# Attention and a two-layer network on one core: twelve Strassen blocks in the first matrix, one sum begun by a copy inside PSUM, nine sums by accumulating DMAs, and another order

## The chip, the core and the metric

The kernel runs on one core of a Trainium2 chip. The core has five engines that run on their own and meet only at semaphores: TensorE (PE; its weight loads are shown as PEld), VectorE (DVE), ScalarE (ACT), GpSimd (POOL) and SyncE (SP). POOL and SP mainly issue DMAs here; a queue issues its DMAs in order, and a DMA that has to wait for a semaphore holds up those behind it on that queue. SBUF is the working memory, PSUM the eight banks into which TensorE writes. The metric is the device time of the whole program in microseconds (us).

## The reference

```python
def _attn_ref(q, k, v, n_global, n_local):        # q, k, v: (4, 8, 768, 64)
    scores = scale * np.matmul(q, k.transpose(0, 1, 3, 2))
    is_global = pos[None, :] < int(n_global)      # the first 8 keys
    is_local = (rel >= 0) & (rel < int(n_local))  # the last 96 keys
    scores = np.where(is_global | is_local, scores + bias, -1000000000.0)
    a = softmax(scores)
    return np.matmul(a, v)

def _moe_ref(x, w_in, w_out):                     # x: (3072, 512)
    h = x @ w_in                                  # w_in: (512, 2048)
    g = h - np.tanh(h)
    return g @ w_out                              # w_out: (2048, 512)
```

Attention with a window of 96 keys and 8 global ones, then two matrices with g = h - tanh(h) between them. The inputs and the output are float32; the kernel computes in bfloat16 with float32 sums in PSUM.

## The kernel before

**Tiles.** The 3072 rows are 24 units u of 128 rows. Per unit: q and k are loaded (lq, lk) and turned (T, Te; from unit 7 on T is a transposing DMA on SP), S makes the scores on TensorE, E their exponentials on ScalarE, M multiplies with a mask on VectorE, AV multiplies with v, R and N divide by the sums, X and Xe (from unit 8 on Xe is a transposing DMA on SP) put the result into xT, the input of the first matrix. K and V copy the global keys and values in.

**First matrix.** Units go in groups g: 0 and 1 of one unit, 2 to 6 of two, 7 to 9 of four, so that a matmul of group 7 to 9 has 512 moving columns. h is made in 16 pieces f of 128 columns of w_in. `m1` (L477) sums a piece over four quarters of x; `th` (L576) takes the tanh on ScalarE and `g` (L590) subtracts on VectorE, into `gall`. For six blocks of groups 8 and 9 (`DUNITS`, L164; a block is four pieces f, j is its number, so j = 1 to 3) the block is made by Strassen's scheme in Winograd's form: seven products d1 to d7 of four 256-column matmuls (`in_product`, L536) instead of four m1 of four 512-column matmuls. v1 to v4 (L509) are the sums of w_in, y1 to y4 (L514) those of x. One PSUM bank ("r") gathers d1, d6, d5 and d3 in turn; after d1, d6 and d5 its state is copied to SBUF (e0, e1, e2, `d_copy`). C11 is d2 in a bank of its own ("q") plus the copy e0, added by VectorE (q11, L547); q21 and q22 (L550) add bank "z" to the other two copies.

**Second matrix.** All twelve pairs of units use the same scheme with seven products p1 to p7 of eight 256-column matmuls (`product`, L645). n1 to n4 (`g_sum`, L630, VectorE) are the sums of g: n1 and n2 go to buffers `ss`, n3 and n4 back into `gall`. a0, a1, a2 (`keep`) copy bank "r" to `sn` after p1, p6, p5; c11, c21, c22 (`result`, L659) add them on VectorE, c12 is a copy; `st` (L662) stores a unit. p7 reads what n3 wrote, p3 what n4 wrote. w1 to w4 (L617) are the sums of w_out. The last pair, 22, has p3 in two halves.

**What sets the order.** `ORDER` (L17) is a list of words, each a step such as `p3.10` (product 3 of the pair that begins with unit 10), `g.8.4` or `n4.16/d`; the letter behind the slash names the engine where there is a choice (a ScalarE, d VectorE, p POOL's queue, s SP's). The program issues the steps in that order (L797 to L806), so that each engine, and each queue, gets its own in the order of the list. `HOMES` (L74) says which buffer or bank each value has. The tile framework adds the waits. The two tables are left out below.

Of the kernel before, what the change touches and what calls it, by code (L numbers as in the profile page):

```python
# [7 lines left out]
FP32 = mybir.dt.float32  # L8
BF16 = mybir.dt.bfloat16
# [32 lines left out]
lk.18 R.12 N.12/d p4.6 th.5.4 lk.19 V.12/a g.5.4 S.12 lq.17 c21.6 p2.8 M.13 E.14.0 st.3.0/p p1.8 lv.14 E.15.0 n1.8/d
AV.13 K.15/d lq.18 n2.8/d a0.8/a m1.6.14 E.14.1 c11.8 lv.15 v2.3 m1.6.4 R.13 K.14/d th.6.14 N.13/d lv.16 p6.8 g.6.14
Xe.13 th.6.4 lq.19 g.6.4 S.13 a1.8/a M.14 p5.8 E.15.1 n4.8/d m1.6.0 E.16.0 T.18 M.15 m1.6.12 a2.8/a th.6.0 T.17 m1.6.8
E.16.1 g.6.0 AV.14 n3.8/d th.6.12 Xe.12 m1.6.10 th.6.8 V.14/d R.14 g.6.12 K.16/a AV.15 g.6.8 m1.6.2 N.14/d p7.8 R.15
th.6.2 N.15/d th.6.10 m1.6.6 c22.8 Xe.15 g.6.2 p4.8 th.6.6 g.6.10 Xe.14 g.6.6 p3.8 c21.8 p1.10 n1.10/d st.9.0/p c12.8/a
T.19 v1.2 lv.17 S.14 n2.10/d a0.10/a V.15/a M.16 lq.20 p2.10 E.17.1 lq.23 p6.10 n4.10/d E.18.0 lv.19 AV.16 a1.10/d
K.17/a E.17.0 m1.7.15 R.16 lk.20 N.16/d p5.10 th.7.15 c11.10 lq.22 g.7.15 m1.7.2 a2.10/a lk.22 v2.2 S.15 th.7.2 lk.21
g.7.2 p3.10 E.19.1 lq.21 n3.10/d m1.7.6 E.18.1 st.5.0/p M.17 m1.7.4 T.20 E.19.0 M.18 m1.7.3 th.7.6 M.19 V.16/a m1.7.5
T.22 th.7.3 m1.7.7 th.7.5 g.7.6 th.7.4 g.7.5 AV.19 th.7.7 m1.7.1 g.7.4 T.21 R.19 v4.3 m1.7.8 N.19/a v3.2 g.7.7 m1.7.12  # L50
g.7.3 th.7.1 m1.7.10 c12.10/d th.7.8 st.10.0/p AV.17 th.7.12 g.7.8 lk.23 m1.7.9 th.7.10 V.17/d R.17 lv.18 N.17/d m1.7.11
th.7.9 g.7.12 Xe.17 K.19/a lv.20 V.19/a m1.7.14 g.7.10 st.7.0/p g.7.9 p7.10 th.7.14 lv.22 g.7.1 th.7.11 m1.7.0 c22.10
lv.21 g.7.14 m1.7.13 th.7.0 T.23 g.7.11 p4.10 g.7.0 th.7.13 Xe.19 g.7.13 S.16 v4.2 p1.12 c21.10 E.20.0 K.21/d n1.12/d
p2.12 K.20/d a0.12/d E.21.0 n2.12/d AV.18 E.20.1 c11.12 p6.12 R.18 N.18/d a1.12/a n1.14/d S.17 Xe.18 n3.12/d p5.12 M.20
E.21.1 Xe.16 p7.12 a2.12/a n4.12/d E.22.0 AV.20 c22.12 p3.12 M.21 E.22.1 p4.12 K.22/a c12.12/a R.20 n2.14/d V.20/a
st.12.0/p S.18 n3.14/d lv.23 p1.14 N.20/d E.23.1 M.22 AV.21 E.23.0 d1.8.1 d2.8.1 y1.8 e0.8.1/a R.21 p2.14 y2.8 a0.14/a
N.21/d V.21/a d6.8.1 y3.8 Xe.21 AV.22 q11.8.1 e1.8.1/a m1.8.0 R.22 c21.12 N.22/d Xe.20 d5.8.1 th.8.0 d7.8.1 c11.14
e2.8.1/a y4.8 d1.8.3 g.8.0 Xe.22 d2.8.3 e0.8.3/a q22.8.1 d3.8.1 d6.8.3 M.23 th.8.4 st.11.0/s d1.8.2 p6.14 e0.8.2/a
n4.14/d V.22/a d6.8.2 g.8.4 e1.8.3/a d2.8.2 e1.8.2/a d4.8.1 q11.8.3 d5.8.3 AV.23 q21.8.1 e2.8.3/a d5.8.2 a1.14/a R.23
q11.8.2 d3.8.3 e2.8.2/a d7.8.3 N.23/d th.8.12 d3.8.2 q22.8.3 Xe.23 p5.14 th.8.6 g.8.12 d7.8.2 a2.14/a st.13.0/s m1.8.2  # L60
q22.8.2 st.8.0/s th.8.8 p3.14 g.8.6 d4.8.3 g.8.8 th.8.2 d4.8.2 c12.14/a m1.9.0 st.14.0/p y1.9 q21.8.3 m1.8.1 g.8.2
th.8.14 d1.9.1 q21.8.2 m1.8.3 e0.9.1/a y2.9 th.8.10 g.8.14 p7.14 d1.9.2 c22.14 th.8.1 d6.9.1 y3.9 d2.9.2 g.8.10 e1.9.1/a
d2.9.1 th.8.3 p4.14 g.8.1 e0.9.2/a g.8.3 d5.9.1 d6.9.2 q11.9.1 p1.16 e1.9.2/a n1.16/d e2.9.1/a d5.9.2 c21.14 a0.16/a
n2.16/d d7.9.1 st.15.0/s th.9.0 d3.9.1 q11.9.2 e2.9.2/a p6.16 th.9.4 g.9.0 y4.9 d3.9.2 a1.16/a g.9.4 m1.9.1 th.9.8
m1.9.2 n1.18/d th.9.1 g.9.8 d1.9.3 p5.16 e0.9.3/a q22.9.1 d6.9.3 n3.16/d d7.9.2 e1.9.3/a d4.9.1 g.9.1 th.9.2 p2.16
q22.9.2 d2.9.3 n2.18/d p1.18 q21.9.1 g.9.2 d4.9.2 a0.18/a d5.9.3 n4.16/d d7.9.3 e2.9.3/a q11.9.3 p7.16 th.9.6 q22.9.3
d3.9.3 c11.16 a2.16/a p6.18 n3.18/d q21.9.2 m1.9.3 g.9.6 p3.16 th.9.3 c22.16 a1.18/a d4.9.3 th.9.12 g.9.3 p5.18 q21.9.3
th.9.10 g.9.12 p4.16 a2.18/a p2.18 g.9.10 th.9.14 p7.18 c12.16/a n4.18/d st.16.0/p p1.20 c22.18 g.9.14 p3.18 a0.20/a
p4.18 n1.20/d n2.20/d p2.20 n3.20/d p6.20 n1.22/d c21.16 p7.20 n4.20/d a1.20/a st.17.0/p p5.20 n3.22/d c21.18 p2.22
c11.18 a2.20/a st.19.0/s n2.22/d c12.18/a p1.22 st.18.0/s c22.20 c11.20 p4.20 a0.22/a c11.22 p6.22 n4.22/d st.22.0/s  # L70
c21.20 p7.22 a1.22/a st.21.0/p p5.22 p3.20 a2.22/a c22.22 p3.22.0 c12.20/a p4.22 st.20.0/s c12.22.0/d st.22.256/s
p3.22.1 c21.22 c12.22.1/d st.23.0/s st.22.384/s
"""
HOMES = """  # L74
v.0:1 tr.0.1:6 tr.0.0:6 kq.0:2 qk.0:6 v.1:0 tr.1.1:6 tr.1.0:7 kq.1:0 qk.1:5 v.2:2 tr.2.1:7 tr.2.0:5 kq.2:1 qk.2:8 v.3:3
tr.3.1:4 tr.3.0:7 kq.3:3 qk.3:7 v.4:4 tr.4.1:3 tr.4.0:1 kq.4:4 qk.4:9 v.5:5 tr.5.1:4 tr.5.0:5 kq.5:0 qk.5:18 v.6:6
tr.6.1:7 tr.6.0:1 kq.6:1 qk.6:4 v.7:4 kq.7:0 qk.7:16 v.8:8 kq.8:1 qk.8:3 v.9:5 kq.9:17 qk.9:2 v.10:6 kq.10:19 qk.10:10
# [44 lines left out]
def kernel(  # L122
# [27 lines left out]
    WJ = 4  # L150
# [692 lines left out]
```

## Time and profile before

| | |
|---|---|
| time, median of 3 runs | 202.13 us (201.87 to 202.61) |
| span of the profiled execution, first to last instruction | 199.8 us |
| TensorE busy | 193.1 us, 2219 matmuls |
| VectorE busy | 178.6 us |
| ScalarE busy | 135.1 us |
| POOL busy | 75.3 us |
| granted TensorE clock | 1.000 |

The profiled execution has a span and no time of its own beside it; the runs' median is 2.3 us above that span, which is what lies around the instructions. In the groups of instructions a row has: line, engine, operation, what it writes and reads with shapes, count | busy time in us, mean length of one in ns | idle time of the engine ahead of it, and who ended that. In a timeline a row has the start and the length in us. The chain of waits is the work that ended last, followed back from the end. In the list of stretches each engine has its busy time and, in brackets, its instructions.

### The profile page before, as it was taken

What the parts mean: (1) busy time and instruction counts of PE and PEld (TensorE: products, weight loads), DVE (VectorE), ACT (ScalarE), POOL (GpSimd) and SP (SyncE); (2) the same over time, 40 slices, a digit from 0 to 9 for tenths busy, and PEclk for the clock granted to TensorE, in tenths of its full rate; (3) what the DMA queues carried; (4) which work ended last, traced back from release to release, by engine and by line L of the source; (5) the groups of instructions that cost most, each with busy time, mean ns of one, the idle gap of its engine ahead of it and who ended that gap; (6) DMA issues with size and microseconds to landing.
All of it is one profiled execution on the core that took longest, in us unless ns stands there. A gap on an engine that the chain in (4) does not pass through costs nothing.

```text
span 199.8 us, 5524 instructions
## 1 busy us (share of the span) xinstructions
PE 193.1 (97%) x2219; PEld 157.8 (79%) x2219; DVE 178.6 (89%) x348; ACT 135.1 (68%) x234; POOL 75.3 (38%) x97
## 2 busy tenths in 40 slices
PE   8799999999999999999999999999999999999992
PEld 2469998888888988988898655688898687888892
DVE  6487599999999999999999898999999999999942
ACT  3698898726569559758947789578778777464220
POOL 8987576350694057069207904702000100001110
PEclk9999999999999999999999999999999999999999
DMA  5999999999999999989996998994733101001233
GB/s 148 211 180 185 198 163 207 201 156 141 193 167 196 178 153 135 133 188 171 137 158 146 140 173 192 154 155 85 55 108 121 66 0 54 3 0 52 107 132 131
DMA packets 103545, 27.36 MB, mean 137 GB/s; under 512 B 93920, under 2 KB 101472, under 8 KB 103520
## 3 DMA queue, kind: packets, MB, share of 16 engines
q0 software_dynamic: 74048, 16.78, 89.5%
q1 hardware_dynamic: 28928, 9.70, 27.6%
q10 hardware_dynamic: 544, 0.52, 1.0%
q8 instruction: 17, 0.28, 0.5%
q14 instruction: 8, 0.07, 0.1%
HBM read 27.26 MB, written 6.29 MB: 168 GB/s over the span
## 4 chain that ended last, share of the span: by engine, by line
PE 85%; DVE 7%; DMA 3%; ACT 2%; issue 1%; ACTq 0%; DVEq 0%
PE ps L645 36%; PE ps L477 27%; PE ps L536 9%; PE ps L396 5%; PE ps L427 5%; DMA f<-in_q_dram 3%; DVE gall L590 2%; DVE x L444 2%; DVE mem L407 1%; PE ps L455 1%; ACT mem L403 1%; PE ps L320 1%; ACT mem L274 1%; PE ps L365 1%; ACT th L576 1%
## 5 line engine op out<-in xcount | busy, mean ns | idle before, releaser
L477 PE MATMUL ps<-xT,w_in_bf 128*128 128x256 bf16 (+2 forms) x544 | 69.0, 279 | 0.0
L477 PEld LDWEIGHTS <-w_in_bf 128*128 128x128 bf16 x544 | 47.2, 98 | 12.4
L576 ACT ACTIVATE th<-ps 128x512 f32<-128x512 f32 (+1 forms) x74 | 41.8, 591 | 18.7 <-PE ps L477 13.6
L590 DVE TENSOR_TENSOR gall<-ps,th 128x512 bf16<-128x512 f32 (+1 forms) x74 | 47.4, 668 | 6.0 <-ACT th L576 5.6
L645 PEld LDWEIGHTS <-gall 128*128 128x128 bf16 x488 | 46.4, 98 | 7.0
L662 POOL DMA_DIRECT2D out_dram<-ot x14 | 8.1, 580 | 102.5 <-ACT ot L274 52.4
L403 ACT ACTIVATE mem<-ps 128x1024 bf16<-128x1024 f32 x44 | 43.3, 1024 | 4.3 <-PE ps L396 4.2
L645 PE MATMUL ps<-w_out_bf,gall 128*128 128x256 bf16 (+1 forms) x296 | 36.3, 270 | 0.0
L274 ACT COPY sn<-ps 128x256 f32<-128x256 f32 x32 | 12.0, 375 | 20.3 <-PE ps L645 16.3
L645 PE MATMUL ps<-f,ss 128*128 128x256 bf16 x192 | 24.9, 273 | 0.0
L645 PE MATMUL ps<-wc,gall 128*128 128x256 bf16 x192 | 24.9, 273 | 0.0
L342 POOL DMA_DIRECT2D vb<-in_v_dram x24 | 21.5, 900 | 2.2 <-issue 1.0
L645 PEld LDWEIGHTS <-ss 128*128 128x128 bf16 x192 | 18.3, 98 | 2.8
L342 POOL DMA_DIRECT2D mem<-in_k_dram x20 | 17.9, 899 | 4.8 <-DMA w_out_bf<-in_moe_w_out_dram 3.1
L342 POOL DMA_DIRECT2D mem<-in_q_dram x20 | 18.1, 904 | 3.8 <-DMA w_out_bf<-in_moe_w_out_dram 3.0
L412 DVE TENSOR_TENSOR mem<-mem,mk 128x2048 bf16<-128x2048 bf16 x16 | 19.2, 1215 | 0.0
L659 DVE TENSOR_TENSOR ot<-ps,sn 128x256 f32<-128x256 f32 x36 | 14.7, 415 | 3.6 <-ACT sn L274 2.5
L444 DVE TENSOR_TENSOR x<-ps,rden 128x512 bf16<-128x512 f32 x23 | 15.8, 687 | 0.5
L274 ACT COPY mem<-ps 128x512 f32<-128x512 f32 (+1 forms) x22 | 12.7, 585 | 5.1 <-PE ps L536 3.9
L427 PEld LDWEIGHTS <-mem 128*128 128x128 bf16 x352 | 13.4, 97 | 2.1 <-ACT mem L403 0.5
L427 PE MATMUL ps<-vb,mem 128*128 128x65 bf16 x352 | 14.7, 193 | 0.0
L396 PE MATMUL ps<-mem 64*128 64x128 bf16 x352 | 13.1, 217 | 0.0
(78 smaller groups left out, 220.7 us busy)
## 6 DMA issues: line engine op xcount, KB each, us to landing
out_dram<-ot POOLq DMA_DIRECT2D x14, 256.0 KB, 2.8
vb<-in_v_dram POOLq DMA_DIRECT2D x24, 128.0 KB, 6.2
mem<-in_q_dram POOLq DMA_DIRECT2D x22, 128.0 KB, 6.3
mem<-in_k_dram POOLq DMA_DIRECT2D x22, 128.0 KB, 6.1
out_dram<-ot SPq DMA_DIRECT2D x9, 256.0 KB, 2.0
w_out_bf<-in_moe_w_out_dram POOLq DMA_DIRECT2D x4, 512.0 KB, 10.7
w_in_bf<-in_moe_w_in_dram POOLq DMA_DIRECT2D x4, 256.0 KB, 7.6
w_in_bf<-in_moe_w_in_dram POOLq DMA_DIRECT2D x2, 512.0 KB, 11.0
```

What stands on the lines that cost most here:

```text
L274: nc.scalar.copy(out=out, in_=in_)
L342: eng(e).dma_start(out=dst, in_=rows_of(src, u).rearrange("h p d -> p h d"))
L396: nc.tensor.matmul(bank(("s", u, o), hh)[:, p * P : (p + 1) * P], buf(("qk", back[u] if o else u))[r, 1, p, :], buf(("qk", u))[r, 0, p, :] ...
L403: nc.scalar.activation(d, banks(("s", u, o), 0, 1), AF.Exp, bias=0.0, scale=scale)
L412: nc.vector.tensor_tensor(out=t, in0=t, in1=mk[:, 1:3], op=ALU.mult)
L427: nc.tensor.matmul(t[:, h // (H // 2), h % (H // 2), :], buf(("p", u, o))[:, slot(h), :], buf(("v", back[u] if o else u))[:, h, 0 : Dh + 1 ...
L444: nc.vector.tensor_tensor(out=buf(("x", u)).rearrange("q (a h) d -> q a h d", a=2), in0=t[:, :, :, 0:Dh], in1=rden.to_broadcast([P, 2, H / ...
L477: nc.tensor.matmul(t[:, (f - f0) * n : (f - f0 + 1) * n], w_in_bf[j][:, c, fo : fo + P], x[:, c, 0:n], start=(c == 0), stop=(c == CD - 1),)
L536: nc.tensor.matmul(t[:, r * 2 * P : (r + 1) * 2 * P], w(r)[:, c], x[:, c], start=first and r + c == 0, stop=c == 1, skip_group_check=not f ...
L576: nc.scalar.activation(h_view(buf(("th", g, f0)), g, m), h_view(bank(("h", g, f0)), g, m), AF.Tanh, bias=0.0, scale=1.0)
L590: nc.vector.tensor_tensor(out=o, in0=v(h), in1=v(th), op=ALU.subtract)
L645: nc.tensor.matmul(bank((holder, a))[:, c0:c1], s(f), t(f)[:, c0:c1], start=first and f == 0, stop=f == HF - 1, skip_group_check=not first,)
```

## The change

**First matrix.** All twelve blocks of groups 7, 8 and 9 are made by seven products; no group of four units has m1 any more (`DUNITS`, groups 7 to 9, j 0 to 3). Two halves of a product's output that belong to one unit now lie together: a matmul writes two runs of 128 columns.

**C11.** In both matrices the copy of bank "r" after the first product goes to bank "q" (PSUM to PSUM, on ScalarE: e0, a0), and product 2 adds onto it in the bank. q11 is gone, c11 is a copy. `q`, `r` and `z` are each a bank with a home of its own.

**Signs and sums.** The sums of g and of w_out are rearranged so that all four of g are additions into one of their operands or a buffer; c21 and c22 subtract instead. Seven n3 and two n4 are issued on POOL's queue as DMAs that add to their destination: n3.8, n3.10, n3.12, n3.14, n3.16, n3.18, n3.20, n4.10 and n4.16, 256 KB each (128 x 1024 bfloat16). The other 39 sums stay on VectorE. `gall` is laid out unit by unit, so that a half of a unit's g is one run.

**Buffers.** `mem` has 20 instead of 23 parts, `xT` 3 instead of 4, `ss` 3 instead of 5; `mk` keeps two masks; the sums of w_in have a tile `ws`.

**Order.** Both tables are new; a line of each as an example.

```diff
 ORDER = """
-c21.20 p7.22 a1.22/a st.21.0/p p5.22 p3.20 a2.22/a c22.22 p3.22.0 c12.20/a p4.22 st.20.0/s c12.22.0/d st.22.256/s
-p3.22.1 c21.22 c12.22.1/d st.23.0/s st.22.384/s
+st.20.0/s p7.22 c22.22 p3.22.0 c12.22.0/d p7.20 p4.22 p3.22.1 c22.20 c21.22 st.23.0/s st.22.256/s st.22.0/p p4.20
+c21.20 st.21.0/s c12.22.1/a st.22.384/p
...
-    DUNITS = [(8, 1), (8, 2), (8, 3), (9, 1), (9, 2), (9, 3)]
+    DUNITS = [(g, j) for g in range(7, 10) for j in range(4)]
...
-    gall = pool.tile([P, NG, CF, 2 * P], BF16, name="gall")
+    gall = pool.tile([P, NG, 2, CF, P], BF16, name="gall")
...
     def d_bank(g, j, part):
-        return bank(("zd", g, j)) if part == "z" else bank(("qr", g, j), 0 if part == "q" else 1)
+        return bank(({"q": "q", "r": "rr", "z": "zd"}[part], g, j))
 
     def d_keep(g, j, k):
-        return buf(("k0", g, j)) if k == 0 else mems(("k12", g, j), FP32)[:, (k - 1) * 4 * P : k * 4 * P]
+        return d_bank(g, j, "q") if k == 0 else mems(("k12", g, j), FP32)[:, (k - 1) * 4 * P : k * 4 * P]
...
-            2: ("q", lambda r: w_in_of(a + r, 2), x_block(g, 2, 1), True),
+            2: ("q", lambda r: w_in_of(a + r, 2), x_block(g, 2, 1), False),
...
-        t = d_bank(g, j, part)
+        t = d_bank(g, j, part).rearrange("q (t r n) -> q t r n", t=2, r=2)
...
-                    t[:, r * 2 * P : (r + 1) * 2 * P], w(r)[:, c], x[:, c], start=first and r + c == 0, stop=c == 1,
+                    t[:, :, r, :], w(r)[:, c], x[:, c], start=first and r + c == 0, stop=c == 1,
...
-        a, b = {1: (b12, b11), 2: (b22, w_half(1, x)), 3: (b22, b12), 4: (b21, w_half(2, x))}[k]
-        nc.vector.tensor_tensor(out=w_half(k, x), in0=a, in1=b, op=ALU.subtract)
+        a, b, o = {
+            1: (b11, b12, ALU.subtract), 3: (b12, b22, ALU.subtract),
+            2: (w_half(3, x), b11, ALU.subtract), 4: (b21, w_half(2, x), ALU.add),
+        }[k]
+        nc.vector.tensor_tensor(out=w_half(k, x), in0=a, in1=b, op=o)
...
-            3: (lambda: a21, lambda: a11, lambda: a21, ALU.subtract),
-            4: (lambda: a12, lambda: a12, lambda: buf(("ss", a, 2)), ALU.subtract),
-        }[k]
-        eng(e).tensor_tensor(out=o(), in0=x(), in1=y(), op=op)
+            1: lambda: (one(), a21, a22), 2: lambda: (two(), one(), a11),
+            3: lambda: (a21, a21, a11), 4: lambda: (a12, a12, two()),
+        }[k]()
+        if e is POOL:
+            nc.gpsimd.dma_start(out=o, in_=y, accum_op=ALU.add)
+        else:
+            eng(e).tensor_tensor(out=o, in0=x, in1=y, op=ALU.add)
...
     def keep(e, a, k):
-        copy(e, buf(("sn", a, k)), bank(("r", a))[:, 0:DH2])
+        copy(e, buf(("sn", a, k)) if k else bank(("q", a))[:, 0:DH2], bank(("r", a))[:, 0:DH2])
...
-        if (i, j) == (1, 2):
-            copy(e, o, bank(("r", a))[:, c0:c1])
+        if i == 1:
+            copy(e, o, bank(("qr"[j - 1], a))[:, c0:c1])
             return
-        holder, k = {(1, 1): ("q", 0), (2, 1): ("z", 1), (2, 2): ("z", 2)}[i, j]
-        nc.vector.tensor_tensor(out=o, in0=bank((holder, a))[:, 0:DH2], in1=buf(("sn", a, k)), op=ALU.add)
+        nc.vector.tensor_tensor(out=o, in0=bank(("z", a))[:, 0:DH2], in1=buf(("sn", a, j)), op=ALU.subtract)
...
-        for w, k in (("q11", 0), ("q21", 1), ("q22", 2)):
+        for w, k in (("q21", 1), ("q22", 2)):
```

What the new order puts on the engines, at three places. First, POOL's queue behind the last loads of k. Before (L342 loads, L662 stores from the buffers ot):

```order
L342 DMA vb2_84<-in_v_dram 128x8x64
L342 DMA vb5_87<-in_v_dram 128x8x64
L662 DMA out_0_dram<-ot0_113 128x512
L342 DMA vb4_86<-in_v_dram 128x8x64
L342 DMA vb6_88<-in_v_dram 128x8x64
L662 DMA out_0_dram<-ot3_116 128x512
L342 DMA vb7_89<-in_v_dram 128x8x64
L662 DMA out_0_dram<-ot3_116 128x512
L662 DMA out_0_dram<-ot0_113 128x512
```

With the change (L344 loads, L671 stores, L638 the sums: gall to gall are n3, ss to gall n4):

```order
L344 DMA mem_81<-in_k_dram 128x8x64
L638 DMA gall_102<-gall_102 128x1024 x2
L638 DMA gall_102<-ss1_104 128x1024
L671 DMA out_0_dram<-ot0_111 128x512
L344 DMA vb2_84<-in_v_dram 128x8x64
L344 DMA vb4_86<-in_v_dram 128x8x64
L671 DMA out_0_dram<-ot3_114 128x512
L671 DMA out_0_dram<-ot2_113 128x512
L638 DMA gall_102<-gall_102 128x1024 x2
L671 DMA out_0_dram<-ot0_111 128x512
L638 DMA gall_102<-ss1_104 128x1024
L638 DMA gall_102<-gall_102 128x1024 x2
```

The sums stand in line with loads and stores: n3.8, n3.10 and n4.10 first, the store of unit 10 and the loads lv.23 and lv.22 behind them; n4.16 ahead of n3.16 and n3.18.

Second, ScalarE around units 6 and 7, where the eighth group of scores, S.8, is next on TensorE. Before (the copy to vb5 is V.5, the two L403 are E.7, the copy to xT2 is Xe.6):

```order
L274 COPY vb5_87<-vb1_83 8x8x64
L274 COPY sn2_110<-ps_61 128x256
L274 COPY sn3_111<-ps_61 128x256
L274 COPY ot2_115<-ps_61 128x256
L403 ACTIVATE mem_81<-ps_61 128x1024 x2
L576 ACTIVATE th_101<-ps_61 128x512
L274 COPY xT2_99<-ps_61 128x4x128
```

With the change (the two L406 are E.7, then V.6, and N.6 as eight scalings, one for each head):

```order
L276 COPY sn2_108<-ps_61 128x256
L580 ACTIVATE th_101<-ps_61 128x512
L406 ACTIVATE mem_81<-ps_61 128x1024 x2
L276 COPY vb4_86<-vb1_83 8x8x64
L443 ACTIVATE x1_95<-ps_61,rden0_115 128x64 x8
L276 COPY ot0_111<-ps_61 128x256
L406 ACTIVATE mem_81<-ps_61 128x1024 x2
```

V.6 and N.6 came from VectorE to ScalarE, between the exponentials of unit 7 and of unit 8. On TensorE AV.6, p3.2, AV.7, p7.2 and S.8 follow one another there (before: AV.6, p4.2, m1.3.14, X.6, p3.0, AV.7, S.8).

Third, the end of VectorE's line (L659 and L668 are c11, c21 and c22, a copy of 128x128 is half of c12.22). Before:

```order
L659 TENSOR_TENSOR ot2_115<-ps_61,sn0_108 128x256
L630 TENSOR_TENSOR gall_102<-gall_102,ss2_105 128x8x128
L659 TENSOR_TENSOR ot1_114<-ps_61,sn3_111 128x256
L659 TENSOR_TENSOR ot0_113<-ps_61,sn0_108 128x256
L276 COPY ot2_115<-ps_61 128x128
L659 TENSOR_TENSOR ot0_113<-ps_61,sn2_110 128x256
L276 COPY ot2_115<-ps_61 128x128
```

With the change:

```order
L278 COPY ot3_114<-ps_61 128x256
L668 TENSOR_TENSOR ot2_113<-ps_61,sn1_107 128x256
L278 COPY ot0_111<-ps_61 128x128
L668 TENSOR_TENSOR ot1_112<-ps_61,sn2_108 128x256
L668 TENSOR_TENSOR ot2_113<-ps_61,sn3_109 128x256
L668 TENSOR_TENSOR ot1_112<-ps_61,sn0_106 128x256
```

VectorE's last step was the second half of c12.22; it is now c21.20, behind p4.20, TensorE's last product, and the second half of c12.22 is on ScalarE. The last store on SP was 128 columns of unit 22 and is now the whole of unit 21; the 128 columns of unit 22 are the last on POOL.

260 lines of the change are left out of this document (132 added, 128 removed).

## The prediction

> **What bounds the kernel now.** I read the page first (engines, clock, chain of waits), then the stretches of 5 us, then TensorE's own waits.
>
> ```profile
> PE 193.1 (97%) x2219; PEld 157.8 (79%) x2219; DVE 178.6 (89%) x348; ACT 135.1 (68%) x234; POOL 75.3 (38%) x97
> PEclk9999999999999999999999999999999999999999
> PE 85%; DVE 7%; DMA 3%; ACT 2%; issue 1%; ACTq 0%; DVEq 0%
> ...
> 5.00:10.00 5.00, 3.79 (x38) 2.12 (x36) 2.27 (x4) 3.26 (x5) 4.83 (x7) 1.00 1.60 211
> 100.00:105.00 5.00, 5.00 (x63) 4.52 (x60) 4.68 (x11) 2.23 (x5) 0.00 (x0) 1.00 1.17 160
> 160.00:165.00 5.00, 5.00 (x49) 4.48 (x47) 5.00 (x9) 3.80 (x9) 0.00 (x0) 1.00 0.00 0
> 180.00:185.00 5.00, 5.00 (x48) 4.49 (x47) 4.93 (x7) 2.06 (x5) 0.56 (x1) 1.00 0.13 52
> ...
> PE ps L455 <- DVE x L444: 0.7, 2, 0.4
> ```
>
> The first three rows are from the page, the next four from the stretches (columns: PE, PEld, DVE, ACT, POOL, granted clock, DMA share, GB/s), the last is TensorE's whole list of waits between 15 and 195 us. After its start TensorE is busy in every stretch at full clock, and the listed waits of its matmuls are 0.7 us in 180. Since a busy PE need not be a PE at its rate, I checked the rate in the chain of waits:
>
> ```profile
> 114.20 4.32 PE ps L477 x20
> 143.74 3.06 PE ps L536 x28
> ```
>
> Twenty 512-column matmuls one behind the other take 4.32 us, 0.216 us each (512 columns); the 28 matmuls of seven Strassen products take 3.06 us, 0.109 us each (256 columns). Both run at the same time per column, so time is TensorE's column count. VectorE is the second limit: 5.00 of 5.00 us from 160 to 165.
>
> **The change, part by part.**
>
> *First matrix.* A block before is four m1 of four 512-column matmuls, 16 x 0.216 = 3.46 us; as seven products it is 28 x 0.109 = 3.06 us. Six more blocks: 6 x (3.46 - 3.06) = **2.4 us less** on TensorE, which is the path. The products now write two runs of 128 columns instead of one of 256; no row of before has that form with a 256-column matmul, so it costs nothing (same columns) or, at most, the gap between the 128-column and the 256-column matmuls' step; I take nothing and keep it as a rival.
>
> *VectorE.* Back to back its instructions start closer together than they last:
>
> ```profile
> 156.26 0.68 DVE L550 TENSOR_TENSOR mem<-ps,mem 128x512 f32<-128x512 f32 x1
> 156.86 0.68 DVE L590 TENSOR_TENSOR gall<-ps,th 128x512 bf16<-128x512 f32 x1
> 157.46 0.68 DVE L550 TENSOR_TENSOR mem<-ps,mem 128x512 f32<-128x512 f32 x1
> 158.06 0.41 DVE L514 TENSOR_TENSOR mem<-xT,mem 128x512 bf16<-128x512 bf16 x1
> 158.39 1.22 DVE L568 TENSOR_TENSOR gall<-mem,th 128x1024 bf16<-128x1024 f32 x1
> 159.52 0.42 DVE L659 TENSOR_TENSOR ot<-ps,sn 128x256 f32<-128x256 f32 x1
> 159.86 0.41 DVE L514 TENSOR_TENSOR mem<-xT 128x512 bf16<-128x512 bf16 x1
> ...
> L630 DVE TENSOR_TENSOR gall<-gall 128x1024 bf16<-128x1024 bf16 x12 | 8.2, 681 | 0.0
> ```
>
> Starts are 0.60 apart for the 0.68 us forms, 0.33 for the 0.41 us, 1.13 for the 1.22 us. In those steps: 24 single g become 12 double ones (-14.4 + 13.6); six q11 go (-3.6); 12 q21/q22 come (+7.2); four sums of w_in and four of x come (+2.7); nine g sums leave (-5.4; L630 lasts as long as L550); eight c11 leave (-2.6); three c12, three of the a and three e2 come (+1.0, +1.0, +1.8); two N and one Te move to ScalarE (-1.8), and five K and two V with them (smaller; -1.0, an estimate). Sum -1.5 us: from 178.6 to 177 in a span 2.4 us shorter, as tight as before, not tighter.
>
> *ScalarE*, by full lengths:
>
> ```profile
> L562 ACT ACTIVATE th<-mem 128x1024 f32<-128x1024 f32 x6 | 6.4, 1059 | 1.4 <-DVE mem L550 1.2 <-DVE gall L568 0.2
> L576 ACT ACTIVATE th<-ps 128x512 f32<-128x512 f32 x70 | 40.2, 602 | 18.7 <-PE ps L477 13.6 <-DVE rden L433 1.9 <-DVE gall L590 1.3
> L274 ACT COPY mem<-ps 128x512 f32<-128x512 f32 x18 | 10.3, 585 | 4.1 <-PE ps L536 3.9
> L274 ACT COPY ot<-ps 128x256 f32<-128x256 f32 x10 | 3.7, 370 | 3.7 <-PE ps L645 3.7
> L274 ACT COPY vb<-vb 8x512 bf16<-8x512 bf16 x10 | 6.1, 606 | 0.0
> L440 ACT ACTIVATE x<-ps,rden 128x64 bf16<-128x64 f32 x8 | 1.8, 330 | 0.5 <-DVE rden L433 0.5
> L274 ACT COPY mem<-mem 128x32 bf16<-128x32 bf16 x9 | 2.0, 218 | 0.0
> L403 ACT ACTIVATE mem<-ps 128x1024 bf16<-128x1024 f32 x44 | 43.3, 1024 | 4.3 <-PE ps L396 4.2
> ```
>
> 24 tanh become 12 double (-1.8), 15 block copies come (+8.8), six fewer copies of kept products and c12 (-2.2), eight c11 (+3.0), two N as eight small scalings each (+3.6), five K, a Te and two V (+1.1, +0.6, +1.2): +14, to 149 of some 198 us, 75%. It still idles a quarter of the time; no cost in the sum.
>
> *The copy inside PSUM.* e0 and a0 used to fill SBUF and VectorE added later; now product 2 adds onto the copy, so TensorE waits for ScalarE there. The copy's row is L274 with 0.585 us (blocks) or 0.37 us (second matrix). No row has PSUM at both ends; bounds: nothing, to twice 0.585. In the first matrix d6 had to wait for e0 before as well. In the second the closest pair has one AV (0.5 us, rows below) between p1.6 and p2.6, against 0.37 for the copy; the others have a product or more. I take nothing.
>
> *Accumulating DMAs.* None is in the trace. Bounds of their landing: the fastest store of the same size below, the slowest load above.
>
> ```profile
> out_dram<-ot POOLq DMA_DIRECT2D x14, 256.0 KB, 2.8
> out_dram<-ot SPq DMA_DIRECT2D x9, 256.0 KB, 2.0
> w_out_bf<-in_moe_w_out_dram POOLq DMA_DIRECT2D x4, 512.0 KB, 10.7
> w_in_bf<-in_moe_w_in_dram POOLq DMA_DIRECT2D x4, 256.0 KB, 7.6
> ...
> 182.22 0.56 POOL L662 DMA_DIRECT2D out_dram<-ot  x1 [25.11 <-ACT ot L274]
> ```
>
> The loads landed at a DMA share above 1.5 (first stretch quoted), the nine sums run where it is mostly under 0.4 (last stretches), so the 2.8 us store is nearest; a sum reads two operands, and I take 4 us, an estimate from that row plus the second read. What matters is the room, in TensorE's steps:
>
> ```profile
> 60.87 0.87 PE ps L645 x8
> 62.61 0.78 PE ps L396 x24
> ...
> 52.79 0.66 PE L427 MATMUL ps<-vb,mem 128*128 128x65 bf16 x16
> 53.29 1.03 PE L645 MATMUL ps<-wc,gall 128*128 128x256 bf16 x8
> ```
>
> A product of the second matrix is 0.87, a group of scores 0.78, an AV 0.50 (from its start to the next), a product of the first 0.44 (3.06 / 7). Tightest is n4.10: it waits for p2.10 and n2.10; TensorE then has S.15, S.16, d7.7.1, d4.7.1, d7.7.3, p6.10, p7.6, p4.6, p5.10 and two AV, 7.3 us, before p3.10; n2.10 ends about 1 us after p2.10 (g.6.14, q21, a double g, n1, c11, n2 stand in line on VectorE), so **6.3 us of room**. n3.16 stands behind n4.16, which waits for p2.16; 14 block products and two of the second matrix follow, 7.9 us, less n4.16 and two issues of 0.56: about 6.8. The others have over 8.5. At 4 us all are hidden. Behind n4.10 on POOL stand st.10 and lv.23, lv.22; st.10 waits for c12.10, which needs p3.10, so those loads are the next to be late.
>
> The Trainium skill ("DMA: Bandwidth & Descriptors", Anatomy of one DMA) gives 2.0 us plus bytes/436e3 for a DMA issued from GpSimd, an estimate of 2.6 us here; the stores' 2.8 us agrees, and by it the sum stays as it is.
>
> *Order.* Moved instructions make new small waits on TensorE and drop old ones. New: S.8 needs the banks that N.6 frees, and N.6 is now on ScalarE behind V.6: 0.61 + 1.8 = 2.4 us, against p3.2, AV.7, p7.2 (0.87 + 0.5 + 0.87 = 2.2): wait 0.2 to 0.6 (one more exp of 1.02 us ahead of it may end late). AV.13 follows S.12 by one product (0.87) where E.14.0 (1.02) must free its bank: 0.2. S.12 and S.17 behind N: 0.1 to 0.2 each. Together 0.9. Dropped: the 0.7 us of L455 waiting for L444 quoted above, since X.5 now has more work ahead of it. Net **+0.2**, bounds -0.7 to +1.2. The start is the same work and the same order of loads on POOL: 0, bounds half a microsecond either way.
>
> *Tail.*
>
> ```profile
> 195.60 0.61 PE L645 MATMUL ps<-w_out_bf,gall 128*128 128x128 bf16 x8
> 196.24 0.29 DVE L276 COPY ot<-ps 128x128 f32<-128x128 f32 x1
> out_dram<-ot SPq DMA_DIRECT2D x2, 64.0 KB, 1.8
> ```
>
> The end was a half product, a 0.29 us copy, a 64 KB store (1.8); it becomes p4.20, a 0.42 us addition and a 256 KB store (2.0): **+0.3**.
>
> Sum against the profiled execution: 199.8 - 2.4 + 0.2 + 0.3 = 197.9 us of span. The runs' median is 202.13, 2.3 above that span; the same 2.3 on top gives **200.2 us**.
>
> **The rivals.**
>
> 1. *A sum lands late* (slower). At p3.10 and p7.16, once a landing passes 6.3 us. Cost: (L - 6.3) + (L - 6.8); the 1.9 us gain is gone at L = 7.5; at 9 us the cost is 4.9, 3.0 more than the gain: about 205 us; at the 10.7 us of the upper row, with n3.20 late too, about 210. For it: both POOL loads of this size or more took 7.6 and 10.7. Against: the idle queues, the stores' 2.8. Chance 0.09.
> 2. *VectorE holds the descriptors back* (slower). Were a POOL issue to wait for a gap of VectorE, n4.16 and n3.16 would wait through stretches that are up to 5.00 of 5.00 busy, some 5 us more each: L about 9, again 205. Against: the store at 182.22 was issued in 0.56 us in a stretch with VectorE 4.93 busy. Chance 0.02. The Trainium skill ("SBUF — State Buffer", Two separate sides) says that VectorE's two-port modes lock GpSimd out of writing descriptors; the row shows no such hold.
> 3. *No change.* ScalarE's 14 us and VectorE's tight line make TensorE wait as long as it gains: four or five places of 0.4 us more than I counted, 201.9 us. For it: VectorE at 5.00 for 20 us on end. Against: its load doesn't grow. Chance 0.16.
> 4. *The split output costs.* 336 matmuls at 10 ns each, 3.4 us: 203.6. Nothing in the trace speaks for it. Chance 0.03.
> 5. *The new order also shortens the stretch from 24 to 35 us*, where the chain runs through VectorE:
>
> ```profile
> 28.96 1.80 DVE gall L590 x3
> ```
>
> n1.0 and Te.6.0 leave VectorE's line there, three small sums of w_in come in; if about half of that piece goes, it is one more microsecond, 199.2. Chance 0.12.
>
> My forecast has the remaining 0.58, with its own range 199.5 to 201.1.
>
> **How the numbers follow.** Half a percent is 1.0 us, about what a measurement here can tell from none: faster is below 201.1, slower above 203.1. Forecast and rival 5 are faster: 0.70; rival 3 is the same: 0.16; rivals 1, 2, 4 are slower: 0.14. The range starts at 199.0 (rival 5) and goes to 203.0, past rival 3 and to the beginning of the late sums; about 0.8 lies in it.
>
> **What would show it.** TensorE's busy time falls by about 2.4 us, 336 matmuls at L540 with starts 0.109 apart; the sums' DMAs land in 3 to 6 us and no matmul waits for a DMA on gall; VectorE stays at about 177 us; waits of a few tenths at L399 (S.8, S.12). It is wrong if TensorE waits on a gall DMA, if L540's step is longer than L536's was, or if idle time of over a microsecond shows on PE beyond 20 us.

## The result, and the profile after

The changed kernel takes 276.94 us, median of 4 runs (273.17 to 280.74); the kernel before, beside it, 202.0 us. The ratio is 1.357 (95% interval 1.345 to 1.370). Some executions fall into a slower state (here 277.65, which is the profiled one, and 280.74), so the ratio, and the savings named below, are taken from the other runs alone, here 276.22 and 273.17 with a mean of 274.7 us. The forecast was 200.2 us, with slower at 0.14: wrong in sign and size.

The rows below are from the page of the changed kernel, the last two from its DMA issues.

```profile
PE 211.7 (77%) x2291; PEld 172.7 (63%) x2291; DVE 180.8 (66%) x332; ACT 149.8 (54%) x263; POOL 81.2 (29%) x103
PEclk9979999799989999999797799979799979999999
...
gall<-gall POOLq DMA_DIRECT2D x7, 256.0 KB, 4.1
gall<-ss POOLq DMA_DIRECT2D x2, 256.0 KB, 3.2
```

The loads of the engines are about what was worked out (VectorE 180.8 us, ScalarE 149.8), and the nine sums land in 3 to 4 us. But no engine is the bound any more: TensorE, busy for 97% before, has 77%, and its clock is no longer full throughout. The stretches show it (columns as before):

```profile
35.00:40.00 5.00, 2.42 (x39) 1.94 (x36) 2.19 (x4) 3.67 (x6) 1.80 (x3) 1.00 1.35 202
45.00:50.00 5.00, 2.39 (x20) 1.88 (x18) 4.96 (x10) 1.64 (x3) 3.92 (x5) 0.93 2.27 153
50.00:55.00 5.00, 5.00 (x35) 3.97 (x34) 1.86 (x4) 2.26 (x5) 2.62 (x3) 0.73 1.85 134
145.00:150.00 5.00, 1.56 (x14) 1.21 (x13) 3.84 (x6) 2.05 (x2) 0.00 (x0) 0.83 0.00 0
150.00:155.00 5.00, 5.00 (x28) 3.47 (x27) 0.99 (x3) 1.75 (x3) 0.00 (x0) 0.50 0.01 3
255.00:260.00 5.00, 5.00 (x48) 4.48 (x46) 4.37 (x5) 3.03 (x6) 0.00 (x0) 1.00 0.16 56
```

In the first row and the fourth (145 to 150) all engines stand for part of the time, so they wait for each other. The fifth is what such a stop costs behind it: 28 matmuls fill 5 us in which 48 go at full clock (last row), at a granted clock of 0.50. The stop ahead of it was 3.44 us long. A stop of 2.61 us, in the second row, is followed by a clock of 0.73 in the third. The Trainium skill ("TensorE: Matmul & The Clock Gate", What's actually happening) says that an idle stretch of some 3.4 us halves TensorE's clock until it has been busy about as long; the stop of 3.44 us agrees, and the one of 2.61 us shows that here less was enough.

So the 76.0 us between the two spans (275.8 - 199.8) divide thus: TensorE idles 275.8 - 211.7 = 64.1 us against 199.8 - 193.1 = 6.7, 57.4 more; and its busy time is 211.7 instead of the 193.1 - 2.4 = 190.7 of the forecast, 21.0 more; 57.4 + 21.0 - 2.4 = 76.0. The lower clock explains at most 16.0 of the 21.0: the mean granted clock of the profiled run is 0.942, and (1 - 0.942) x 275.8 = 16.0. The other 5 us aren't accounted for with certainty. One part, an estimate: four block matmuls are counted as busy for 0.60 us while the next four start 0.44 us behind them, so each stop leaves up to 0.16 us more counted as busy, and the list of TensorE's waits has some 50 stops.

What its matmuls wait for (the head of the list of waits):

```profile
PE ps L540 <- DVE gall L571: 8.9, 5, 3.4
PE ps L655 <- ACT mem L406: 6.7, 5, 2.4
PE ps L480 <- ACT mem L406: 6.4, 3, 2.6
PE ps L480 <- DVE x L447: 4.1, 4, 1.7
PE ps L655 <- ACT ps L276: 3.6, 3, 1.7
```

L655 is a product of the second matrix, L480 an m1, L406 the exp of a group of scores. Neither matmul reads what that exp writes, and in the longer of these waits neither has one of its two banks: at 79.32 us p1.4 (bank 4) waits for an exp on banks 1 and 7, at 71.92 us p4.2 (bank 3) for another on banks 1 and 7. A timeline around unit 5 shows the same on ScalarE:

```profile
33.02 0.62 PE L398 MATMUL ps<-mem 64*128 64x128 bf16 x16
33.91 0.68 DVE L595 TENSOR_TENSOR gall<-ps,th 128x512 bf16<-128x512 f32 x1
34.46 0.65 PE L430 MATMUL ps<-vb,mem 128*128 128x65 bf16 x16
34.68 1.02 ACT L406 ACTIVATE mem<-ps 128x1024 bf16<-128x1024 f32 x1 [0.96 <-DVE gall L595]
36.35 0.20 DVE L436 RECIPROCAL rden<-ps 128x8 f32<-128x8 f32 x1
36.58 1.02 ACT L406 ACTIVATE mem<-ps 128x1024 bf16<-128x1024 f32 x1 [0.87 <-DVE rden L436]
```

The scores of unit 5 (S.5, first row) are done at 33.64. Their exps start at 34.68 and 36.58, each just behind an instruction of VectorE that has nothing to do with them: a subtraction g and the reciprocal R.4. The table of homes says what they share. In the changed kernel the scores of unit 5 lie in banks 1 and 3 and in banks 4 and 6, the h that g reads in bank 2, and the AV that R.4 reads in banks 5 and 7. An exp reads its two banks with one instruction (`banks()`: `ps[:, x : y + 1 : y - x, :]`, a step from bank x to bank y). In the kernel before every such pair was (0,1), (2,3), (4,5) or (6,7).

### The profile page after: what moved, and what is told of

The parts are those of the page before. It is cut to its first block, busy times and chain, and to the rows that moved or that the text cites. A ratio compares the mean times of both kernels' runs of the same rounds, so it can differ in the third digit from the quotient of the medians.

```text
span 275.8 us, 5688 instructions
## 1 busy us (share of the span) xinstructions
PE 211.7 (77%) x2291; PEld 172.7 (63%) x2291; DVE 180.8 (66%) x332; ACT 149.8 (54%) x263; POOL 81.2 (29%) x103
## 3 DMA queue, kind: packets, MB, share of 16 engines
q0 software_dynamic: 75024, 18.03, 70.3%
## 5 line engine op out<-in xcount | busy, mean ns | idle before, releaser
L655 PEld LDWEIGHTS <-gall 128*128 128x128 bf16 x488 | 48.3, 102 | 22.4 <-issue 15.1
L480 PE MATMUL ps<-xT,w_in_bf 128*128 128x256 bf16 (+1 forms) x448 | 50.7, 266 | 12.4 <-ACT mem L406 6.4
L406 ACT ACTIVATE mem<-ps 128x1024 bf16<-128x1024 f32 x44 | 44.0, 1023 | 14.3 <-PE ps L398 7.6
L480 PEld LDWEIGHTS <-w_in_bf 128*128 128x128 bf16 x448 | 39.5, 101 | 19.3 <-issue 14.2
L655 PE MATMUL ps<-w_out_bf,gall 128*128 128x256 bf16 (+1 forms) x296 | 40.2, 285 | 8.0 <-ACT mem L406 2.4
L595 DVE TENSOR_TENSOR gall<-ps,th 128x512 bf16<-128x512 f32 (+1 forms) x50 | 31.7, 659 | 15.5 <-ACT th L580 13.6
L580 ACT ACTIVATE th<-ps 128x512 f32<-128x512 f32 (+1 forms) x50 | 28.3, 584 | 20.6 <-PE ps L480 18.8
L655 PE MATMUL ps<-wc,gall 128*128 128x256 bf16 x192 | 25.5, 279 | 5.3 <-DVE x L447 3.1
L655 PE MATMUL ps<-f,ss 128*128 128x256 bf16 x192 | 24.6, 272 | 5.9 <-ACT ps L276 2.2
L540 PE MATMUL ps<-mem,ws 128*128 128x256 bf16 x144 | 21.6, 280 | 8.8 <-DVE gall L571 5.3
L540 PEld LDWEIGHTS <-ws 128*128 128x128 bf16 x192 | 18.8, 99 | 15.4 <-issue 11.6
L344 POOL DMA_DIRECT2D vb<-in_v_dram x24 | 21.3, 894 | 20.7 <-PE ps L430 10.0
L671 POOL DMA_DIRECT2D out_dram<-ot x11 | 6.3, 576 | 67.3 <-DVE ot L668 24.6
L655 PEld LDWEIGHTS <-ss 128*128 128x128 bf16 x192 | 18.6, 98 | 9.0 <-issue 6.5
L276 ACT COPY ps<-ps 128x256 f32<-128x256 f32 (+1 forms) x24 | 11.1, 469 | 22.1 <-PE ps L540 11.2
L638 POOL DMA_DIRECT2D gall<-gall x7 | 6.4, 1000 | 54.2 <-DVE ss L640 54.2
L571 DVE TENSOR_TENSOR gall<-ps,th 128x1024 bf16<-128x1024 f32 x12 | 14.7, 1224 | 10.6 <-ACT th L565 8.4
L550 DVE TENSOR_TENSOR mem<-ps,mem 128x512 f32<-128x512 f32 x24 | 16.3, 684 | 8.0 <-PE ps L540 7.9
L540 PEld LDWEIGHTS <-w_in_bf 128*128 128x128 bf16 x144 | 15.9, 111 | 7.9 <-issue 4.3
L344 POOL DMA_DIRECT2D mem<-in_k_dram x20 | 17.8, 894 | 8.5 <-ACT mem L276 5.5
L344 POOL DMA_DIRECT2D mem<-in_q_dram x20 | 18.0, 900 | 6.9 <-PE ps L430 4.2
## 6 DMA issues: line engine op xcount, KB each, us to landing
w_out_bf<-in_moe_w_out_dram POOLq DMA_DIRECT2D x4, 512.0 KB, 10.7
```

The costliest lines, as they stand in the source:

```text
L276: nc.scalar.copy(out=out, in_=in_)
L344: eng(e).dma_start(out=dst, in_=rows_of(src, u).rearrange("h p d -> p h d"))
L406: nc.scalar.activation(d, banks(("s", u, o), 0, 1), AF.Exp, bias=0.0, scale=scale)
L480: nc.tensor.matmul(t[:, (f - f0) * n : (f - f0 + 1) * n], w_in_bf[j][:, c, fo : fo + P], x[:, c, 0:n], start=f == f0 and c == 0, stop=(c = ...
L540: nc.tensor.matmul(t[:, :, r, :], w(r)[:, c], x[:, c], start=first and r + c == 0, stop=c == 1, skip_group_check=not first or r > 0,)
L550: nc.vector.tensor_tensor(out=a, in0=d_bank(g, j, "z"), in1=a, op=ALU.add)
```

## The theories

**A.** An instruction that reads two banks is ordered by the tile framework against everything from its first to its last address, the banks between included, reads of another engine too. With pairs up to seven banks apart, the list's order decides who waits for whom among steps that share nothing. **B.** The accumulating DMAs land late (rival 1). **C.** The copy inside PSUM puts ScalarE between two products. **D.** The order of the steps is bad in itself.

## The experiments

**Pairs of banks side by side** (`near`). The list of steps is untouched; only homes of PSUM change; the pairs of scores and AVs, and q with rr of a block, always get neighbours (words picked from the table):

```diff
-s.4.0:0,4 s.4.1:5,7  s.5.0:4,6 s.5.1:1,3  s.9.0:1,7  av.4:5,7 av.5:4,6
+s.4.0:6,7 s.4.1:4,5  s.5.0:5,6 s.5.1:0,1  s.9.0:1,2  av.4:3,4 av.5:5,6
```

> The changed kernel, its list of steps untouched; only the PSUM banks in the table of homes are placed anew, so that the two banks of a group of scores, of an AV and of a block's C11 and C12 always lie side by side (in the changed kernel they are up to seven apart: scores of unit 9 in banks 1 and 7). Theory A: one instruction that reads two banks is ordered by the tile framework against whatever lies in the banks between them too, so exp, R and N wait for, and hold up, matmuls that they share no data with. A expects 199 to 206 us. B (accumulating DMAs land late), C (the copy inside PSUM puts ScalarE between two products) and D (the order of the steps is bad) expect 270 to 280, since all three are still in it.

231.44 us, ratio 1.145 (1.140 to 1.150). Six tenths of the loss are gone (43 of 73 us), which B, C and D don't allow; but A's 199 to 206 is missed by 25 us, so there is a second cause. This kernel and `near_time` leave something out: in six (here) and three (there) blocks or pairs the bank of q was last an AV's or a half-width product's, and product 2 overwrites the copy instead of adding to it. The instructions are the same. (The Trainium skill, "PSUM — Partial Sum Buffer", The four PSUM rules: a matmul without the start flag adds only where a hidden bit is set, and a start clears the bits of its whole bank. No trace here shows the bit itself.) The later kernels keep q off such banks.

**The kernel before with pairs four apart** (`far_before`). Bank 2k becomes k, bank 2k+1 becomes k+4, nothing else:

```diff
-s.4.0:6,7 s.4.1:4,5 av.4:0,1 xt.4:0
+s.4.0:3,7 s.4.1:2,6 av.4:0,4 xt.4:0
```

> The kernel before with its eight banks renamed: bank 2k becomes k, bank 2k+1 becomes k+4. Every pair of banks that lay side by side is now four apart; same instructions, same order, same true dependencies. Theory A expects well over 230 us, with waits of TensorE for exp (L403) and VectorE at places where it waited for nothing. B, C and D expect 202, since nothing that they name is in it.

276.85 us, one run. A table of bank numbers alone makes the kernel before as slow as the changed one, without any of the change's blocks, DMAs or copies. Its list of waits (L399 is exp, L473 an m1, L423 an AV, L641 a product of the second matrix):

```profile
PE ps L473 <- ACT mem L399: 13.1, 12, 2.2
PE ps L423 <- ACT mem L399: 7.2, 9, 1.8
PE ps L473 <- DVE gall L564: 3.9, 3, 2.9
...
PE ps L641 <- ACT mem L399: 2.5, 4, 0.9
```

m1 waits for exp twelve times, where the kernel before had two waits in all beyond 15 us.

**The nine sums on VectorE** (`sums_dve`).

```diff
-n3.8/p n3.10/p n4.10/p n3.12/p n3.14/p n4.16/p n3.16/p n3.18/p n3.20/p
+n3.8/d n3.10/d n4.10/d n3.12/d n3.14/d n4.16/d n3.16/d n3.18/d n3.20/d
```

> The changed kernel with its nine sums of g on VectorE instead of accumulating DMAs; all else as it is. B expects the loss to go: 200 to 206 us. A, C and D expect 270 to 285.

279.90 us, one run: B is out.

**Banks side by side and the list in time order** (`near_time`).

> The changed kernel with its banks placed side by side as in the first run of this group, and its list of steps written in the order in which the steps can start, each engine's own order kept but for steps of equal time. Theory A expects 198 to 205 us, within 2 us of the first run. D expects this to be the run in which the loss goes, with the first still at 270 or more. B and C expect 270 to 280.

229.62 us, one run, 1.8 from `near`: D is out as the cause of the 43 us, and what is left isn't the list's order across engines. TensorE's own order is that of the changed kernel here, as in every version below but `best3`, so whether that order costs part of the rest stays open. C has no run of its own: none takes the copy out of the changed kernel. `near` keeps it and loses 43 us less, and `far_before` is slow without it.

**The two-bank instructions cut in two** (`cut`, and `cut_e` for exp alone). Here the banks stay as the change has them, and only the reach of an instruction changes; R, N and the blocks' tanh and subtraction likewise in `cut`:

```diff
-        nc.scalar.activation(d, banks(("s", u, o), 0, 1), AF.Exp, bias=0.0, scale=scale)
+        for a in range(2):
+            nc.scalar.activation(d[:, a], bank(("s", u, o), a), AF.Exp, bias=0.0, scale=scale)
```

> The changed kernel with all its banks, orders and DMAs as they are; only the instructions that read two banks (exp, R, N on VectorE, the tanh and the subtraction of a block's C11 and C12) are each written as two that read one bank. That adds about 44 + 48 + 22 + 24 fixed parts of 0.1 to 0.2 us on ScalarE and VectorE, which have room. Theory A (a two-bank instruction is ordered against what lies between the banks) expects the waits of TensorE for exp at lines that don't use it to go, and the time to fall to what the kernel with banks side by side had, 225 to 235 us; what is left then is a second cause, TensorE's scores waiting for transposing DMAs. If the banks' placing had helped for another reason, cutting changes nothing or adds its fixed parts: 277 to 290.

> As the run before in this group, but only the 44 exps are cut in two; R, N and the blocks' tanh and subtraction still read two banks. Theory A expects part of the loss to go, 255 to 268 us, between the changed kernel and the run with all of them cut, since the other three kinds still reach over the banks between. If only exp mattered, it would be the same as all cut, 225 to 235.

228.94 us (ratio 1.135, 1.130 to 1.139) and 261.53 us (one run), both where A had them. This is the sharpest of the runs: it adds 56 instructions on ScalarE and 57 on VectorE, and takes off 46 us. That it is the framework that sets these waits, by the span of addresses, is inferred from such times; its code was not read. What TensorE waits for in `cut`:

```profile
PE ps L398 <- DMA mem<-mem: 13.4, 5, 6.3
PE ps L672 <- DVE ot L685: 3.2, 1, 3.2
PE ps L367 <- DMA mem<-in_q_dram: 1.3, 1, 1.3
...
PE ps L431 <- ACT mem L407: 0.3, 1, 0.3
```

Exp (L407) has all but left the list. In its place the scores (L398) wait for the transposing DMAs (T), which no matmul did in the changed kernel.

**The second cause: DMAs in the wrong order.** All have adjacent banks in placings that keep q's rule; the list is untouched in `near_ok` and `near2`, and in `near_loads` and `near2_loads` only DMAs stand elsewhere in it: loads, sums and stores on POOL's queue, and on SP's the transposing DMAs and stores.

> The changed kernel with its list of steps untouched and all its pairs of banks side by side once more, in another placing: no block's or pair's q (where product 2 adds onto the copy) takes a bank that an AV, a transpose or a half-width product used last. It is the reference for the next two. Theory A with the second cause (A2: the POOL queue issues loads of late units early and they crowd out the ones TensorE waits for) expects what the run with the instructions cut in two had, 225 to 235 us, with TensorE's scores (L397) waiting 12 to 18 us for transposing DMAs.

> As the run before it, with the same banks and the same order on TensorE, VectorE and ScalarE; only DMAs stand at other places in the list: on POOL's queue loads of units that are needed late (lv.16 to lv.21, lq.18, lq.19, lk.23) go behind those needed next, and on SP's queue T.23 goes from before T.17 to behind T.21. A2 expects 213 to 222 us, with the waits of the scores for transposing DMAs down by at least two thirds. If the DMAs are simply too many for this order (all are needed earlier than before), it expects no gain from their order: 225 or more. If the DMA waits only hide waits for VectorE or ScalarE that come out behind them, 225 or more too, with those in the list of waits.

> Pairs of banks side by side, DMAs placed anew as in the run before and the list in the order in which steps can start. A2 expects 208 to 218 us: still slower than the kernel before, since this order of TensorE asks for the scores of units 13 to 18 up to 14 us earlier than before.

230.33 us, 229.33 (ratio 1.139, 1.133 to 1.146) and 224.37 (1.115, 1.109 to 1.121). The time of `near_ok` was as expected and its reason was not; A2's 213 to 222 and 208 to 218 were missed. The list of waits of `near_ok`:

```profile
PE ps L539 <- DVE x L446: 6.1, 1, 6.1
PE ps L479 <- DVE gall L594: 4.2, 3, 2.4
PE ps L479 <- ACT mem L405: 3.5, 3, 1.6
```

No score waits for T in it: this placing of banks is so tight that m1 waits for ScalarE and VectorE to free them, which comes first. So it was no reference for A2 (that the placing is what makes them wait is argued from this list). Besides, `near_loads` also moved DMAs of the first 40 us and lost time there: in its first 20 us the granted clock was 0.69 instead of 1.00, and S.4 started at 34.2 us instead of 27.9. From S.4 to the end `near_loads` takes 193.3 us and `near_ok` 201.7, so the new places may have gained some 8 us behind the start; but a late start also leaves the loads more time. These three settle nothing about A2, and the question was put again, with a looser placing and the list up to some 41 us left alone (only the words of POOL's loads and of SP's queue are shown):

```diff
 lq.7 lk.7 lq.9 lk.9
-lq.8 lk.8 lv.6 lk.12 lq.10 lk.10 lv.7 lq.18 lq.12 lk.13 lq.11 lk.11 lk.23 lv.9 lv.8 lv.11
+lv.9 lk.8 lq.11 lk.13 lk.12 lk.23 lk.11 lq.8 lv.7 lq.10 lk.10 lv.8 lv.6 lq.12 lq.23 lv.10
...
-T.16 Xe.10 Xe.12 st.0.0/s T.23 T.17 Xe.11 T.18
+T.17 Xe.10 T.16 Xe.11 Xe.12 T.18 st.0.0/s Xe.13 T.20 Xe.14 Xe.15 T.22 T.23
```

> The changed kernel, its list of steps untouched, pairs of banks side by side in a third placing that leaves TensorE fewer bank waits than the second and follows the same rule for q. A2 (loads crowd each other out once the banks no longer hold TensorE back) expects 225 to 233 us: TensorE's lag behind its own work grows little up to the scores of unit 8 (S.8, at some 56 us), then by 25 to 30 us up to 140 us, and stays from there on. If bank waits were still at work, the lag would also grow behind 140 us.

> As the run before it with the same banks and engine orders; DMAs stand at other places in the list, this time only those that come later than some 42 us, so that the start is untouched (the first try at this moved early ones too and lost 6 us there). A2 expects 208 to 220 us, the lag between S.8 and 140 us down to 8 to 18 us. If the order simply needs more bytes by then than the queues move, it expects 225 or more.

> As the run before it, with the list in the order in which steps can start, another placing of banks side by side and its own placing of the later DMAs. A2 expects 206 to 220 us; that it would beat the kernel before (under 201) is not expected.

230.80 us (1.142, 1.138 to 1.146), 218.08 (1.079, 1.076 to 1.082) and 219.71 (1.089, 1.083 to 1.095): as A2 had them. In `near2`, TensorE's waits for DMAs from the timeline, and three rows of the DMA issues (median us to landing):

```profile
59.61 0.40 PE L397 MATMUL ps<-mem 64*128 64x128 bf16 x8 [2.87 <-DMA mem<-mem]
72.59 0.61 PE L397 MATMUL ps<-mem 64*128 64x128 bf16 x8 [2.56 <-DMA mem<-mem]
91.29 0.85 PE L397 MATMUL ps<-mem 64*128 64x128 bf16 x24 [2.95 <-DMA mem<-mem]
117.40 0.61 PE L397 MATMUL ps<-mem 64*128 64x128 bf16 x8 [4.41 <-DMA mem<-mem]
...
vb<-in_v_dram POOLq DMA_DIRECT2D x24, 128.0 KB, 9.8
mem<-in_q_dram POOLq DMA_DIRECT2D x22, 128.0 KB, 10.5
mem<-mem SPq DMA_TRANSPOSE x17, 9.2
```

and in `near2_loads`, the same rows and the waits for DMAs that are left:

```profile
vb<-in_v_dram POOLq DMA_DIRECT2D x24, 128.0 KB, 6.7
mem<-in_q_dram POOLq DMA_DIRECT2D x22, 128.0 KB, 6.3
mem<-mem SPq DMA_TRANSPOSE x17, 5.2
...
59.70 1.04 PE L426 MATMUL ps<-vb,mem 128*128 128x65 bf16 x16 [5.03 <-DMA vb<-in_v_dram]
64.78 0.84 PE L394 MATMUL ps<-mem 64*128 64x128 bf16 x24 [0.62 <-DMA mem<-mem]
```

The same transfers, in another order, land in 5.2 us instead of 9.2 (medians of T; the three rows of the kernel before are 6.2, 6.3 and 5.4), and the waits for T shrink from 14.4 us to 0.6; one wait came in their place, for a v that I had put too far back. Both queues were changed at once: late loads went back on POOL, and on SP T.23 went from before T.17 to behind T.22. How much is due to loads that crowd each other, as A2 has it, and how much to a T that stands behind a late one on SP, these runs don't separate.

TensorE has the same order in the next four kernels, so the starts of its steps can be set side by side (us, from the traces):

| step | changed | `cut` | `near2` | `near2_loads` |
|---|---|---|---|---|
| S.8 | 67.7 | 57.6 | 56.1 | 64.8 |
| S.14 | 122.7 | 109.2 | 112.0 | 106.6 |
| S.16 | 170.3 | 147.9 | 148.5 | 135.1 |
| p1.20 | 255.3 | 207.0 | 208.1 | 195.5 |

The reach of the two-bank reads costs time in every stage: the changed kernel is 10.1 us behind `cut` at S.8, 13.5 at S.14, 22.4 at S.16 and 48.3 at p1.20. The order of the DMAs costs it in the middle: from S.8 to S.16 `near2` takes 92.4 us and `near2_loads` 70.3, and behind S.16 both take 60 (`cut` 59.1, the changed kernel 85.0). `near2_loads` gave back 8.7 of the 22 us ahead of S.8: 5.0 of them in the wait for v, and 3.0 ahead of S.4 (26.5 us against 23.5), where its list is still that of `near2` and `loads_dve`, with the same list there, has 23.6. The profile of the changed kernel is 3.0 us longer than the mean of 274.7, so its column may be late by as much towards the end. And why did no matmul wait for T in the changed kernel? It reached S.14 10.7 us later than `near2`: the first cause had hidden the second.

**What is left, and what the DMAs that add are worth** (`loads_dve`, `best3`). `loads_dve` is `near2_loads` with n3 and n4 back on VectorE, by the diff of `sums_dve`.

> The kernel with banks side by side and its later DMAs placed anew (218.1 us), with its nine sums of g on VectorE at the same places of the list instead of accumulating DMAs. It asks whether those DMAs were worth anything once the two causes are out of the way. If VectorE is the second limit in the last 80 us, as the prediction had it, nine sums of 0.60 us more on it cost 2 to 5 us: 220 to 223. If VectorE has room there (the time lost earlier doesn't come back), it stays at 217.5 to 219. If the DMAs were late in places, it falls below 217.

> Banks side by side in another placing, later DMAs and some steps behind 30 us placed anew once more, mainly so that v of unit 6 lands in time (its AV waited 5.0 us) and the scores of S.12 and S.13 find their banks free (3.0 us). The two causes expect most of these 8 us to go: 208 to 215 us. If there is a third cause in the middle of the run, it stays at 216 to 220.

222.36 us (ratio 1.102, 1.099 to 1.105) against 218.08: the accumulating DMAs save 4.3 us once TensorE isn't held elsewhere. The loss lies where the sums stand: both traces have S.15 at 131 us (131.3 and 131.5), and from there to the end `loads_dve` takes 90.0 us and `near2_loads` 84.4. The engines' rows, first with the DMAs, then without:

```profile
PE 197.0 (91%) x2291; PEld 166.9 (77%) x2291; DVE 178.2 (83%) x332; ACT 147.6 (68%) x263; POOL 81.4 (38%) x103
```

```profile
PE 197.3 (89%) x2289; PEld 166.1 (75%) x2291; DVE 183.7 (83%) x341; ACT 147.7 (67%) x263; POOL 73.3 (33%) x94
```

5.5 us more on VectorE, 4.3 us more in all. `best3` took 216.60 us in one run and 221.65 to 223.51 in three others, one of which its trace shows. There AV.6 no longer waits for v. By the run of 216.60 it is 1.5 us better than `near2_loads`, but not in the 208 to 215 that was expected; it lies in the 216 to 220 that the expectation gave to a third cause.

What the last 16 us to the kernel before consist of is therefore only partly known. By the profiles (215.9 and 199.8 us) TensorE idles 18.9 us in `near2_loads` against 6.7, and is busy 3.9 more, at a clock of 0.976. Its list of waits names 5.0 us for that v, 3.0 for N on VectorE and 1.4 for a load of q. Behind S.4 `best1` is the shortest of all, 184.2 us against 189.4 in `near2_loads` and 176.3 in the kernel before; it lost that again by its late start (S.4 at 38.1 us), which may also have helped its loads. No version tried here beats the kernel before.

## Why the prediction was wrong

*The step that failed* is "Order … Net +0.2, bounds -0.7 to +1.2". It counted waits between steps that share data or a bank, of which there are few, as the small numbers there say. It did not ask over which addresses the framework takes an instruction to reach. The banks' new homes, which the prediction passed over as a table, put pairs apart; that cost 44 to 46 us (changed against `near2` and `cut`), and `far_before` shows that it alone costs 75 us in the kernel before. None of the five rivals named it.

*A second step* is in the same paragraph: "The start is the same work and the same order of loads on POOL: 0". For the start that holds in `near2` (S.4 at 23.5 us, as before), but the loads behind the start weren't looked at. The new order issues loads of late units among urgent ones (lk.23 and lq.18 ahead of S.8; before, ahead of S.16 and S.13); 12.7 us hang on the order of the DMAs alone (`near2` against `near2_loads`).

*First matrix, 2.4 us less.* The rate is as predicted. From the chain of waits of the changed kernel:

```profile
233.33 2.63 PE ps L540 x24
```

24 matmuls in 2.63 us, 0.110 each; so the form with two runs of 128 columns costs nothing (rival 4 is out). Whether 2.4 us come off a full TensorE, no run shows.

*VectorE 177, ScalarE 149.* 180.8 and 149.8 in the changed kernel, 178.2 and 147.6 in `near2_loads`. VectorE's sum was 1 to 4 us short.

*The copy inside PSUM, nothing extra.* Right. Two rows of the groups, shapes kept apart:

```profile
L276 ACT COPY ps<-ps 128x512 f32<-128x512 f32 x12 | 6.9, 577 | 14.6 <-PE ps L540 11.2 <-DVE mem L550 2.5 <-DVE gall L571 0.9
L276 ACT COPY ps<-ps 128x256 f32<-128x256 f32 x12 | 4.3, 360 | 7.5 <-PE ps L655 3.7 <-DVE x L447 2.4 <-DVE gall L571 1.3
```

0.577 and 0.360 us, the length of the copies to SBUF (0.585 and 0.370). The 3.6 us that TensorE waited for it in the changed kernel are not in the head of the lists of `cut` or `near2`.

*Accumulating DMAs, 4 us, hidden.* Right in size (4.1 and 3.2) and in effect: no matmul waits for a DMA on gall, and `loads_dve` puts their worth at 4.3 us. Rivals 1 and 2 are out. The upper row of the bounds wasn't the slowest load on POOL: two of 512 KB (w_in) took 11.0 us in the kernel before; nothing hangs on it.

*Waits of tenths at S.8 and S.12.* The one at S.8 came as forecast, 0.37 us for N.6 on ScalarE (`PE ps L398 <- ACT x L443: 0.4, 1, 0.4` in the changed kernel's list), within 0.2 to 0.6; but N.6 had itself waited 2.1 us for VectorE, so that the size fits is luck. S.12 waited 0.88 us for N on VectorE, not 0.1 to 0.2.

*Tail, +0.3.* From the end of TensorE's last matmul to the end of the span it is 3.6 us before, 3.7 in the changed kernel and 3.6 in `near2_loads`: +0.1 at most.

## What to carry to other kernels

Before costing a new placing of buffers, ask of each instruction with a step over banks or slots what lies between its first and last address: it may be ordered against all of that, and a list that isn't in time order then sets who waits. Cutting such an instruction in two is a cheap test, and here a net gain of 46 us. When a stall goes, look at what was hidden behind it: the order of DMAs that was early enough for a slow kernel made them late in a fast one.

## What was not expected of the hardware

A stop of TensorE is paid twice: to 57 us of added idle time come up to 16 us from matmuls at a lower clock, and a stop of 2.61 us was long enough for it. The order of the same transfers alone set how long each takes to land: a 128 KB load of q 6.3 us or 10.5, and a transposing DMA 5.2 or 9.2 (medians). Whether that is the number of them in flight wasn't measured.
